# Holding back projections and starting products early in a planned order for a two-layer attention and GEGLU block

## The chip, the cores and the metric

The kernel runs on one core of one Trainium2 chip. The metric is the device time of one execution in microseconds (us), as the median of several runs. The profiled execution is a single one, taken by the hardware profiler, and its page gives a span from the first to the last instruction, a little shorter than the execution's time. Engines: PE is TensorE's matmul, PEld its weight load, DVE VectorE, ACT ScalarE, POOL GpSimd, SP SyncE (which here issues DMAs).

## The reference

Two layers over 2048 tokens of width 512, each an attention with a running memory followed by a GEGLU feed-forward. Both layers use the same weights.

```python
def _A_ref(x, wq, wk, wv, wo, beta):            # H = 32 heads of 16, N = 4 segments of L = 512 tokens
    q, k, v = ...                               # x @ wq, x @ wk, x @ wv, split by head and segment
    phi = lambda t: jnp.where(t > 0, t + 1.0, jnp.exp(t))
    g = _sigmoid(beta).reshape(1, H, 1, 1)
    M, z = 0, 0
    for s in range(N):
        p = _softmax(einsum('bhqd,bhkd->bhqk', qs, ks) * scale + mask)   # causal inside the segment
        a_dot = einsum('bhqk,bhkd->bhqd', p, vs)
        a_mem = (phi(qs) @ M) / (phi(qs) @ z + 1e-06)
        outs.append(g * a_mem + (1.0 - g) * a_dot)
        M = M + einsum('bhld,bhle->bhde', phi(ks), vs)
        z = z + phi(ks).sum(over l)
    return concat(outs) @ wo

def _B_ref(x, w_gate, w_up, w_down):            # F = 1792
    return _gelu(x @ w_gate) * (x @ w_up) @ w_down

x = A_x
for _ in range(2):
    x = x + _A_ref(_layernorm(x), A_wq, A_wk, A_wv, A_wo, A_beta)
    x = x + _B_ref(_layernorm(x), B_w_gate, B_w_up, B_w_down)
```

## The kernel before

The work is cut into eight pieces, called segments 1 to 8 here: segments 1 to 4 are the four segments of layer 1, 5 to 8 those of layer 2. In the code segment n has k = n - 1. Each runs through two classes. `Att(k)` makes the layer norm of its 512 tokens (tile `xnT`, the normed tokens transposed), the q, k and v products, the scores in 36 rounds, their exponentials, the products of probabilities and v (called flushes), and what the memory needs (`phi`, `mem`, `upd`). `Ffn(k)` makes the Wo product and adds it to x, the second layer norm, 14 gate tiles, 14 up tiles and the down product.

A product on TensorE is four matmuls over the four blocks of 128 of the contraction (14 for down), each with up to 512 columns, into one of eight PSUM banks (tile `ps`). Scores use TensorE in row tiles (four head groups at once), flushes in column tiles (four groups of 32 output columns). A dense product can be whole or cut in four column tiles, so that it can follow a flush without a change of tiling; a matmul in column tiles is then four instructions that run side by side.

The order of everything is made in advance, when the program is built. `order()` walks along a planned clock (`ck`), on which each engine has a time at which it is free. It keeps a list of items: an `Item` has a due time, a condition (`ready`) on what must be there by then, the matmuls to be issued (`ops`), and what follows on other engines (`done`). At each step the main loop does the first of these that it can: two score rounds, if ScalarE's list of exponentials runs low and two bank pairs are free; the next matmul of the item that is open; open the ready item with the least due time; score rounds regardless of ScalarE's list; a fill product of the constant tile `warm`; let 0.05 us pass on the planned clock. Each engine then runs its queue in that fixed order, with semaphores for what it needs from others, so on the chip a late operand holds up everything behind it on the same engine.

Due times, preferences and thresholds are numbers in the table `POLICY`, changed every 20 us of the planned clock by `STAGES`. Those that matter here: `quick`, for how many of the four token blocks after Wo the addition to x also gives the row sum, with the squares then summed on ScalarE (`Norm.added`, L750 to L757), in place of `bn_stats` on VectorE (L737); `turn_pe`, whether normed blocks are transposed by TensorE (L426, tiles `ident` and `xn`, then a copy out of PSUM) or by a DMA (L635); `direct`, how many gate tiles go through GELU straight from PSUM (L1385) rather than being copied to `gel_sb` first (L660 on ScalarE, L659 on VectorE) and put through GELU in place (L1468).

Nearly all matmuls are recorded at one line, L422. In the profile they are told apart by what they read: `wq_sb`, `wk_sb`, `wv_sb`, `aT,wo_sb`, `wg_sb` (gate), `wu_sb` (up), `gel_sb,wd_sb` (down), `q` with `kf` or `kx` (scores), `pt` with `vaug` or `vz` (flush). The exponentials are L1716 on ScalarE. From a flush to Wo, VectorE reads out and transposes (L1266), takes reciprocals (L1276), scales (L1282) and transposes back into `aT` (L1289); L1292 adds the memory's part. From Wo to the gates the path is: addition to x (L1338), statistics (L737, L740), one over the deviation (L777 and L783 on ScalarE or L775 and L780 on GpSimd), scaled block `xn` (L801), transpose into `xnT`.

Of the kernel before, what the change touches and what calls it, by code (L numbers as in the profile page):

```python
# [21 lines left out]
NSEG = 4  # L22
NK = 2 * NSEG
L = 512
# [41 lines left out]
def table(halved):  # L66
# [17 lines left out]
    if halved:  # L84
# [31 lines left out]
    rs_pool=2.183, f_urge=-172.366, quick=0, paired=2, turn_pe=1, turn_last=0, w_at=31.878, w_gap=1.658,  # L116
    wd_at=82.393, wd_gap=1.568, flush_wait=-24.125, piece_slack=54.103, kb_slack=137.385, mem_slack=-57.872,
    margin=0.5, qk_due=0.997, e_q=-0.936, e_k=1.44, exp_slack=-54.603, e_slack=89.377, phi_slack=25.941,
    gelu_slack=-0.515, act_evict=7.804, first_evict=59.504, gate_step=5.742, up_due=-13.195, up_step=36.193,
    down_due=-11.638, down_step=-8.082, upd_due=2.96, kb_act=13.215, vz_slack=-3.085, x_dve=18.716, v0_due=-19.099,  # L120
    x1_at=-0.749, x2_at=17.766, x3_at=25.618, x3_load=-134.921, direct=4, gelu_tiles=6, look=1.24, lag=0.479,
    wv_at=-163.476, xn_pool=70.356, kb_pool=58.307, cut_pool=-1.34, at_pool=-24.815, pe_turns=0, gate_due=-25.221,
    shun=2.375, col_gap=3.222, hold=14, early=1.718, starve=0.315, near=7.532, cap=8, soon=2.605, columns=0,
    kd_slack=-7.947, zero_slack=-2.858)
# [3 lines left out]
        f_urge=-142.106, turn_pe=0, kb_slack=136.166, e_q=-0.628, upd_due=0.734, gelu_tiles=4, cut_pool=-1.244)),  # L128
    (2, 3, dict(
        rs_pool=2.062, f_urge=-142.106, turn_pe=2, flush_wait=-23.401, kb_slack=132.867, qk_due=-4.716, e_q=-0.628,  # L130
        phi_slack=25.306, gelu_slack=3.249, act_evict=-10.809, down_due=-8.472, down_step=-19.183, upd_due=2.131,
        kb_act=8.112, vz_slack=-2.427, gelu_tiles=3, look=1.351, xn_pool=81.967, kb_pool=58.345, cut_pool=-1.308,
        at_pool=-4.617, gate_due=-26.901, shun=4.857, early=1.703, starve=0.32, near=7.708, soon=2.65)),
    (3, 4, dict(
        rs_pool=2.062, f_urge=-142.106, turn_pe=2, flush_wait=-23.401, kb_slack=132.867, qk_due=-4.716, e_q=-0.628,
        phi_slack=25.306, gelu_slack=3.249, act_evict=-10.809, gate_step=6.048, up_step=48.132, down_due=-8.472,
        down_step=-19.183, upd_due=2.131, kb_act=8.112, vz_slack=-2.427, x_dve=-17.494, gelu_tiles=3, look=1.351,
        xn_pool=81.967, cut_pool=-1.308, at_pool=-4.617, gate_due=-3.182, shun=4.857, hold=10, early=1.703,
        starve=0.32, near=7.708, cap=9, soon=2.65)),
    (4, 5, dict(  # L140
        rs_pool=6.739, f_urge=-142.106, quick=1, turn_pe=4, flush_wait=-25.073, piece_slack=89.739, kb_slack=132.867,
        mem_slack=-58.782, qk_due=-65.306, e_q=-0.628, e_k=5.331, exp_slack=-31.237, phi_slack=25.306,
        gelu_slack=3.249, act_evict=-10.809, gate_step=5.036, up_due=-0.982, up_step=0.332, down_due=-8.472,
        down_step=-19.183, upd_due=16.794, kb_act=1.607, vz_slack=-2.427, x_dve=-2.16, look=1.351, lag=0.415,
        xn_pool=-0.079, cut_pool=-1.491, at_pool=20.04, gate_due=10.318, shun=3.803, hold=10, early=1.703,
        starve=0.338, near=6.791, cap=12, soon=30.667)),
    (5, 6, dict(
        rs_pool=7.71, f_urge=-142.106, quick=1, paired=1, turn_pe=4, flush_wait=-32.146, piece_slack=89.739,
        kb_slack=132.746, mem_slack=-59.02, qk_due=-65.538, e_q=-0.535, e_k=5.331, exp_slack=-31.237,
        phi_slack=25.29, gelu_slack=3.249, act_evict=-10.809, gate_step=5.036, up_due=-0.982, up_step=0.332,  # L150
        down_due=-8.472, down_step=-18.931, upd_due=16.794, kb_act=-3.437, vz_slack=-2.427, x_dve=-2.16, direct=6,
        look=1.351, lag=0.415, xn_pool=-0.079, cut_pool=-1.491, at_pool=24.384, gate_due=1.419, shun=3.803, hold=9,
        early=1.703, starve=0.338, near=6.791, cap=13, soon=30.667)),
    (6, 7, dict(
        rs_pool=-35.334, f_urge=-142.106, quick=6, paired=1, turn_pe=8, flush_wait=-3.829, piece_slack=-11.221,
        kb_slack=105.872, mem_slack=73.299, qk_due=-8.214, e_q=-7.15, e_k=84.404, exp_slack=0.985, phi_slack=36.681,
        gelu_slack=139.816, act_evict=-10.809, gate_step=5.036, up_due=-0.571, up_step=0.208, down_due=74.558,
        down_step=-6.986, upd_due=-1.601, kb_act=120.49, vz_slack=-45.689, x_dve=6.382, gelu_tiles=7, look=2.788,
        lag=0.247, xn_pool=9.373, cut_pool=1.514, at_pool=24.384, gate_due=-0.563, shun=101.359, hold=11,
        early=1.703, starve=59.91, near=-2.703, cap=6, soon=-12.515)),  # L160
    (7, 8, dict(
# [292 lines left out]
def order(pol, nc, cst, seg, wrk, psp, A_x, A_wq, A_wk, A_wv, A_wo, A_beta, B_x, B_w_gate, B_w_up, B_w_down, out):  # L454
# [412 lines left out]
    class Att:  # L867
# [977 lines left out]
```

## Time and profile before

| | |
|---|---|
| median of 3 runs | 538.32 us (537.79 to 538.46) |
| profiled execution | 537.38 us |
| its span | 535.7 us |
| granted TensorE clock, mean | 1.000 |
| instructions on TensorE in the profile | 10403 matmuls, 10462 weight loads |
| exponentials on ScalarE (L1716) | 288, busy 280.2 us |
| multiplication of gate and up on VectorE (L1409) | 112, busy 74.3 us |
| SP's queue | 52 transposes of `xn`, 14 copies of `vaug` into `vz` |

How to read it: a group's line gives line, engine, operation, tiles, shapes and count, then busy time and the mean duration of one in ns, then idle time of the engine ahead of them with what ended most of it. A timeline line gives start, length, engine, line, operation, tiles, shapes and count of merged instructions, with idle time before them in brackets where there is some. A matmul's record lasts until its result is out, and the next one starts well before that, so the distance of starts is the time that a matmul takes from TensorE, not the record's length. A few matmul records are missing from the trace.

### The profile page before, as it was taken

The numbers are of one execution on the slowest core, as the hardware profiler recorded it, in microseconds if no ns is written. First come the engines' busy times: TensorE is split into PE (matmuls) and PEld (weight loads), VectorE is DVE, ScalarE is ACT, GpSimd is POOL, SyncE is SP. The second block draws the span as 40 slices with busy tenths as digits, with TensorE's granted clock in tenths as the row PEclk, the third lists the DMA queues.
The fourth block names the chain that finished last, engine by engine and source line by source line (L and its number), as shares of the span: only waits on it lengthen the run. The fifth ranks groups of instructions, "written<-read, shape, count | busy, mean of one in ns | idle before, by whom it ended". The sixth has DMA issues, their size and how long they took to land.

```text
span 535.7 us, 23633 instructions
## 1 busy us (share of the span) xinstructions
PE 518.7 (97%) x10403; PEld 272.4 (51%) x10462; DVE 438.7 (82%) x834; ACT 438.9 (82%) x589; POOL 275.2 (51%) x343
## 2 busy tenths in 40 slices
PE   8999989999999999999999999999999999999997
PEld 4455455545554445544555445444565456556554
DVE  7987998998888999888999899879887897685342
ACT  7999999989999889998699986998899978942320
POOL 2977585467872968727677167513563155300000
PEclk9999999999999999999999999999999999999999
DMA  8378841152121123310323123101230114003001
GB/s 267 70 101 207 183 130 33 23 64 50 23 53 31 24 42 53 61 24 2 72 42 62 24 42 62 23 0 23 61 64 2 23 32 82 15 2 71 12 2 42
DMA packets 74586, 29.46 MB, mean 55 GB/s; under 512 B 58866, under 2 KB 74482, under 8 KB 74482
## 3 DMA queue, kind: packets, MB, share of 16 engines
q1 hardware_dynamic: 74192, 27.67, 25.5%
q8 instruction: 82, 1.34, 1.0%
q10 hardware_dynamic: 290, 0.26, 0.1%
q14 instruction: 22, 0.18, 0.1%
HBM read 9.70 MB, written 2.10 MB: 22 GB/s over the span
## 4 chain that ended last, share of the span: by engine, by line
PE 85%; DVE 9%; issue 2%; ACT 2%; DMA 0%; POOL 0%; DVEq 0%; POOLq 0%
PE ps L422 84%; ACT pt L1716 2%; DVE byq L1266 1%; DVE x_sb L1338 1%; DVE e L1026 1%; DVE ab L1282 1%; DVE st L737 1%; DVE pt L1675 1%; DMA x_sb<-in_A_x_dram 0%; PE ps L426 0%; DVE gel_sb L1409 0%; DVE r L1276 0%; DVE aT L1289 0%; DVE st L1501 0%; DVE vaug L659 0%
## 5 line engine op out<-in xcount | busy, mean ns | idle before, releaser
L1716 ACT ACTIVATE pt<-ps 128x1024 bf16<-128x1024 f32 x288 | 280.2, 1036 | 37.9 <-PE ps L422 31.7
L1665 POOL TENSOR_SCALAR_AFFINE_SELECT pt<-pt 128x256 bf16<-128x256 bf16 (+1 forms) x192 | 111.5, 594 | 143.1 <-ACT pt L1716 127.3
L422 PE MATMUL ps<-xnT,wg_sb 128*32 128x512 bf16 (+1 forms) x1143 | 105.6, 380 | 2.0 <-issue 1.1
L422 PE MATMUL ps<-wd_sb,gel_sb 128*32 128x512 bf16 (+2 forms) x1486 | 102.4, 353 | 1.8 <-issue 1.6
L422 PE MATMUL ps<-xnT,wu_sb 128*32 128x512 bf16 (+1 forms) x1188 | 100.8, 379 | 1.3 <-issue 1.1
L1409 DVE TENSOR_TENSOR gel_sb<-gel_sb,ps 128x512 bf16<-128x512 bf16 x112 | 74.3, 683 | 25.7 <-PE ps L422 22.7
L422 PEld LDWEIGHTS <-gel_sb 128*32 128x32 bf16 (+1 forms) x1689 | 53.5, 97 | 40.8 <-issue 1.5
L422 PEld LDWEIGHTS <-wu_sb 128*32 128x32 bf16 (+1 forms) x1198 | 44.6, 97 | 46.9 <-issue 0.9
L422 PEld LDWEIGHTS <-wg_sb 128*32 128x32 bf16 (+1 forms) x1156 | 43.0, 97 | 42.8 <-issue 0.7
L1266 DVE STREAM_TRANSPOSE byq<-ps 128x512 f32<-128x512 f32 x64 | 45.1, 706 | 17.4 <-PE ps L422 17.0
L1045 POOL TENSOR_SCALAR e<-e 128x512 bf16<-128x512 bf16 x34 | 52.9, 1558 | 2.7 <-ACT e L1022 2.0
L1338 DVE TENSOR_TENSOR x_sb<-x_sb,ps 128x512 bf16<-128x512 bf16 (+1 forms) x59 | 37.1, 639 | 20.5 <-PE ps L422 19.7
L1670 POOL TENSOR_SCALAR_AFFINE_SELECT pt<-pt 64x1024 bf16<-64x1024 bf16 x38 | 45.8, 1205 | 11.2 <-ACT pt L1716 7.0
L422 PE MATMUL ps<-pt,vaug 128*32 128x256 bf16 (+2 forms) x1344 | 34.9, 238 | 0.8 <-POOL pt L1665 0.5
L1468 ACT ACTIVATE gel_sb<-gel_sb 128x512 bf16<-128x512 bf16 (+4 forms) x42 | 35.3, 928 | 0.0
L422 PE MATMUL ps<-xnT,wq_sb 128*32 128x512 bf16 (+2 forms) x261 | 34.3, 377 | 0.8 <-issue 0.5
L737 DVE BATCH_NORM_STATS2 st<-x_sb 128x6 f32<-128x512 bf16 x51 | 34.5, 677 | 0.1
L422 PE MATMUL ps<-xnT,wk_sb 128*32 128x512 bf16 (+2 forms) x263 | 33.4, 376 | 1.0 <-issue 0.5
L659 DVE CAST gel_sb<-ps 128x512 bf16<-128x512 f32 x45 | 30.0, 679 | 4.9 <-PE ps L422 4.5
L422 PEld LDWEIGHTS <-vaug 128*32 128x32 bf16 x1344 | 27.4, 97 | 10.2 <-issue 1.8
L422 PE MATMUL ps<-wv_sb,xnT 128*32 128x512 bf16 (+1 forms) x223 | 30.9, 380 | 0.7 <-issue 0.5
L422 PE MATMUL ps<-q,kx 32*128 32x64 bf16 (+2 forms) x1120 | 31.1, 217 | 0.5 <-ACT pt L1716 0.4
(128 smaller groups left out, 701.6 us busy)
## 6 DMA issues: line engine op xcount, KB each, us to landing
vz<-vaug SPq DMA_DIRECT2D x14, 136.0 KB, 2.9
wg_sb<-in_B_w_gate_dram SPq DMA_DIRECT2D x8, 224.0 KB, 4.4
wu_sb<-in_B_w_up_dram SPq DMA_DIRECT2D x8, 224.0 KB, 3.5
wd_sb<-in_B_w_down_dram SPq DMA_DIRECT2D x7, 256.0 KB, 5.8
x_sb<-in_A_x_dram SPq DMA_DIRECT2D x3, 512.0 KB, 7.2
out_dram<-x_sb SPq DMA_DIRECT2D x12, 128.0 KB, 1.9
xnT<-xn SPq DMA_TRANSPOSE x52, 2.5
kx<-kf SPq DMA_DIRECT2D x12, 64.0 KB, 4.4
```

Of the source, the lines that this page charges most:

```text
L422: self.nc.tensor.matmul(*args, **kw)
L659: ck.dve.post(ck.made(), slack, (0.673, lambda: nc.vector.tensor_copy(out=dst(), in_=src()), end), taken=taken)
L737: nc.vector.bn_stats(out=self.st6[:, 0, :], in_=x_sb[:, self.tt0 + j, :])
L1026: nc.vector.scalar_tensor_tensor(out=dst, in0=src, scalar=0.0, in1=e[0][:], op0=ALU.max, op1=ALU.add, accum_out=self.zk[:, b:b + 1] if whi ...
L1045: lambda eng: eng.tensor_scalar(out=e[0][:], in0=e[0][:], scalar1=1.0, scalar2=None, op0=ALU.min), summed)
L1266: nc.vector.transpose(out=(self.byq[:, pars[0], :, :].rearrange("p a c -> p (a c)") if h is None else self.byq[:].rearrange("p u a c -> p ...
L1338: ck.dve.post(ck.made(), slack, (0.15 + 0.00104 * (c1 - c0), lambda: nc.vector.tensor_tensor(out=xt, in0=xt, in1=ps()[:, 0:c1 - c0], op=AL ...
L1409: ck.dve.post(ck.made(), NORMAL, (0.683, lambda: nc.vector.tensor_tensor(out=g, in0=g, in1=ps()[:], op=ALU.mult), lambda t: (ps.read(t), e ...
L1468: return (0.205 + 0.427 * (f1 - f0), lambda: nc.scalar.activation(out=g, in_=g, func=ACT.Gelu_apprx_tanh), lambda t: self.gelu_done(t, f0, ...
L1665: nc.gpsimd.affine_select(out=view, in_=view, pattern=[[0, 4], [0, n], [1, C]], compare_op=ALU.is_ge, fill=0.0, base=C, channel_multiplier=-1)
L1670: nc.gpsimd.affine_select(out=view, in_=view, pattern=[[0, 4 * TPS], [1, C]], compare_op=ALU.is_ge, fill=0.0, base=0, channel_multiplier=-1)
L1716: nc.scalar.activation(out=pt_all[:, s0:s0 + 2, 2 * p:2 * p + 2, :].rearrange("p r h c -> p h r c"), in_=ps_all[:, pair[0]:pair[1] + 1, :] ...
```

## The change

Four things change. First, the q and k items of segments 2 to 4 (`0 < k < NSEG`) are not ready before a given round of scores has been issued, and neither are their v items; the round is set by `hold1`, `hold2`, `hold3` for the segment, `hold_step` for the block, and `hold_v` more for v. Second, a Wo item can be begun when three of its four head blocks are there, once all scores of its segment are issued: three matmuls now, the item is then parked with its bank, and the last matmul follows when the fourth block is there. Third, a gate item can be begun when the first two token blocks of `xnT` are there: four matmuls on 256 columns, the item is parked, and four more on the other 256 columns follow. Both are tried only where no item is ready and no score round can be issued, that is where the loop came to a fill before, and at most `park` items are parked. Parked items go on ahead of any other. Fourth, all numbers of `POLICY` and `STAGES` are new, with a stage for nearly each 20 us.

```diff
 POLICY = dict(
-    rs_pool=2.183, f_urge=-172.366, quick=0, paired=2, turn_pe=1, turn_last=0, w_at=31.878, w_gap=1.658,
...
+    kd_slack=-5.85, zero_slack=-1.031, hold1=-49.923, hold2=2.205, hold3=11.541, hold_step=-162.485, hold_v=23.995,
+    park=3)
...
+        self.early, self.rest, self.stop = None, None, 0
...
+            def begun_by(j, more=0.0):
+                if not 0 < k < NSEG:
+                    return True
+                now = STEPS * streams[0][0] + streams[0][1] if streams else 1e9
+                return now >= (0.0, pol.hold1, pol.hold2, pol.hold3)[k] + pol.hold_step * j + more
...
-                return Item(lambda: k - pol.qk_due + 0.01 * b, lambda: storage() and ck.has(("xnTa", k)), dense(ps, pairs),
+                return Item(lambda: k - pol.qk_due + 0.01 * b, lambda: storage() and begun_by(b) and ck.has(("xnTa", k)), dense(ps, pairs),
...
-                            lambda: ck.has(("xnTa", k, j)) and (k or ck.pe > max(pol.wv_at, 13.4)) and
+                            lambda: ck.has(("xnTa", k, j)) and begun_by(j, pol.hold_v) and (k or ck.pe > max(pol.wv_at, 13.4)) and
...
+                def early():
+                    if ("scores", k) in ev and soon(("aTh", k, j // 2), KT - 1, eager=True):
+                        it.stop = 1
+                        return True
+                    return False
+
+                it.early, it.rest = early, lambda: ck.has(("aTh", k, j // 2, KT - 1), by=ck.pe - 0.1)
...
+                def early():
+                    if not (ck.has(("xnTf", k, 0), ("xnTf", k, 1)) and free()):
+                        return False
+                    it.ops[:] = [(Clocks.MM[512] / 2, lambda i=i, l=l, r=r, c=c: product(ps()[:, c], l(), r()[:, c], i == 0, i == KT - 1))
+                                 for c in (slice(0, L // 2), slice(L // 2, L)) for i, (l, r) in enumerate(pairs)]
+                    it.stop = KT
+                    return True
+
+                it.early, it.rest = early, lambda: ck.has(("xnTf", k))
...
-            if not opened.ops:
+            if len(opened.ops) == opened.stop:
                 it, opened = opened, None
-                it.done()
+                if it.ops:
+                    parked.append(it)
+                else:
+                    it.done()
+            continue
+        got = [it for it in parked if it.rest()]
+        if got:
+            opened = got[0]
+            opened.stop = 0
+            parked.remove(opened)
             continue
...
+        if bank is not None and len(parked) < pol.park:
+            got = [it for it in sorted((it for it in items if it.early), key=lambda it: it.due())[:6] if it.early()]
+            if got:
+                opened = open_item(got[:1], bank)
+                continue
```

What the built programs hold, by count of instructions:

| | before | after |
|---|---|---|
| fill products after the start (whole / in column tiles) | 25 / 20 | 11 / 8 |
| transposing matmuls of `xn` on TensorE | 48 | 32 |
| transposes of `xn` by DMA | 52 | 56 |
| gate matmuls on 256 columns (whole / in column tiles) | 0 / 0 | 31 / 196 |
| changes of TensorE's tiling along its queue | 298 | 294 |
| additions to x with a row sum, squares on ScalarE | 9 | 14 |
| products read out into `gel_sb` by ScalarE, GELU or copy | 68 | 76 |
| v tiles read out into `vaug` by ScalarE / VectorE | 9 / 19 | 16 / 12 |
| GELU in place on ScalarE (instructions / tiles) | 42 / 70 | 31 / 68 |

All other products have the same number of columns in total. Three Wo items of segment 2 and three of segment 8 are begun on three head blocks, and ten gate items, in segments 3 and 4, on 256 tokens.

More of the change, by code (lines that the diff above doesn't have):

```diff
@@ L1393, in done, with free @@
                         self.gelu_all(ck.pe)
-                return Item(lambda: -0.8 if phase[0] == k else k + pol.gate_due + pol.gate_step * place(ft),
-                            lambda: ck.has(("xnTf", k), ("loaded", "first")) and (k == 0 and ft >= HELD or (("down", k - 1) if k else ("upd", 0)) in ev),
-                            dense(ps, pairs), done, kind="gate", ps=ps, after=("xnTf", k))
+                def free():
+                    return ck.has(("loaded", "first")) and (k == 0 and ft >= HELD or (("down", k - 1) if k else ("upd", 0)) in ev)
+                it = Item(lambda: -0.8 if phase[0] == k else k + pol.gate_due + pol.gate_step * place(ft),
+                          lambda: ck.has(("xnTf", k)) and free(),
+                          dense(ps, pairs), done, kind="gate", ps=ps, after=("xnTf", k))
+                def early():
[6 more added lines that the diff above has]
+                it.early, it.rest = early, lambda: ck.has(("xnTf", k))
+                return it
             def up(ft):
@@ L1592, in order @@
     streams = [(k, t) for k in range(NK) for t in range(STEPS)]
-    opened = None
+    opened, parked = None, []
     score_banks = set()
```

288 lines of the change are left out of this document (203 added, 85 removed).

## The prediction

> **What bounds the kernel now.** I read the page first, then busy time by stage, then TensorE's instructions in order of time where the stages showed idle time. The page's lines on the span, the busy shares, the granted clock and the chain that ended last:
>
> ```profile
> span 535.7 us, 23633 instructions
> PE 518.7 (97%) x10403; PEld 272.4 (51%) x10462; DVE 438.7 (82%) x834; ACT 438.9 (82%) x589; POOL 275.2 (51%) x343
> PEclk9999999999999999999999999999999999999999
> PE 85%; DVE 9%; issue 2%; ACT 2%; DMA 0%; POOL 0%; DVEq 0%; POOLq 0%
> ```
>
> TensorE holds 85% of the chain and runs at full clock in every slice. In 17.0 us of the span (535.7 less 518.7) no matmul is running. The profiled execution took 537.38 us, 1.7 us more than its span; the median of the three runs is 538.32, 0.94 above it. I work out a difference on the profiled execution and apply it to the median. About 0.2%, 1.1 us, is the smallest difference that a measurement of this kernel can tell from none.
>
> Busy time by stage:
>
> ```profile
> 20.00:40.00 20.00, 19.01 (x369) 9.60 (x374) 17.16 (x40) 20.00 (x28) 16.66 (x24) 1.00 0.61 89
> 60.00:80.00 20.00, 17.77 (x407) 10.05 (x406) 19.40 (x40) 18.59 (x24) 13.95 (x19) 1.00 0.58 136
> 100.00:140.00 40.00, 37.92 (x828) 19.90 (x823) 36.98 (x75) 35.95 (x54) 30.46 (x32) 1.00 0.27 39
> 140.00:180.00 40.00, 39.22 (x843) 20.71 (x848) 33.85 (x63) 39.27 (x50) 23.96 (x28) 1.00 0.18 36
> ```
>
> The columns after the length are PE, PEld, DVE, ACT, POOL. TensorE is idle for 2.23 us in 60 to 80 and 2.08 us in 100 to 140, and hardly elsewhere. In 60 to 80 VectorE is busy for 19.40 of 20; ScalarE is full in 20 to 40 and nearly so (39.27 of 40) in 140 to 180. So TensorE bounds the kernel, with two places where it waits, and ScalarE stands close behind it.
>
> Busy shares flatter TensorE, because a record runs on after the next matmul has started. So I read starts. TensorE's timeline at those places; `ps<-warm` are the fill products, put in where the planner has no work ready:
>
> ```profile
> 63.50 0.33 PE L422 MATMUL ps<-warm 128*128 128x128 bf16 x3
> 63.76 0.41 PE L422 MATMUL ps<-q,kx 32*128 32x64 bf16 x20
> ...
> 70.18 0.28 PE L422 MATMUL ps<-warm 128*32 128x128 bf16 x8
> ...
> 71.28 0.40 PE L426 MATMUL ps<-ident,xn 128*128 128x128 bf16 x4
> ...
> 72.04 0.23 PE L422 MATMUL ps<-warm 128*128 128x128 bf16 x1
> 72.40 0.40 PE L426 MATMUL ps<-ident,xn 128*128 128x128 bf16 x4
> 72.63 0.42 PE L422 MATMUL ps<-warm 128*128 128x128 bf16 x4
> ...
> 73.64 0.29 PE L422 MATMUL ps<-q,kf 16*128 16x64 bf16 x8
> ...
> 75.27 0.62 PE L426 MATMUL ps<-ident,xn 128*128 128x128 bf16 x8
> 75.72 0.33 PE L422 MATMUL ps<-warm 128*128 128x128 bf16 x3
> ...
> 76.47 1.02 PE L422 MATMUL ps<-xnT,wg_sb 128*128 128x512 bf16 x3
> ...
> 107.81 1.03 PE L422 MATMUL ps<-xnT,wu_sb 128*128 128x512 bf16 x4 [0.16 <-issue]
> 108.67 0.44 PE L422 MATMUL ps<-warm 128*128 128x128 bf16 x5
> 109.04 0.28 PE L422 MATMUL ps<-q,kx 32*128 32x256 bf16 x2
> 109.75 0.40 PE L422 MATMUL ps<-q,kx 32*128 32x256 bf16 x10 [0.42 <-ACT pt L1716]
> ...
> 134.93 0.39 PE L422 MATMUL ps<-warm 128*128 128x128 bf16 x4
> ...
> 135.78 0.38 PE L422 MATMUL ps<-xnT,wg_sb 128*128 128x512 bf16 x1 [0.46 <-ACT xnT L660]
> ```
>
> From the first fill of each stretch to the next useful start I read 0.26, 1.10, 0.36, 1.01, 0.75, 0.37 and 0.85 us: 4.70 us in which TensorE does nothing of use. Of the program's 30 fills (25 whole, and 20 instructions that make five groups of four) 29 lie in these stretches, so a fill stands for 0.162 us of dead time. The stretches from 70 to 76 are the layer norm after the first Wo products: their blocks wait for VectorE.
>
> **The change part by part.** *Dead time.* The new order has 13 fills (11 whole, two groups). The v products of segment 4 now stand behind the first Wo products, where before only fills and scores stood, and VectorE's chain there loses two statistics. Sixteen v products are 16 x 0.215 = 3.4 us of cover (four matmuls from 107.81 to 108.67), against the 3.48 us of dead time up to 76.47. In segment 2 the q, k and v products of segment 5 take the place of the fills at 134.93. At 0.162 each, 17 fewer fills give **-2.8 us**. Ends: -4.7 if all dead time goes, 0 if each wait stays and only its fill goes.
>
> *Transposes.* TensorE turns 48 blocks of 128 columns before and 32 after. Eight of them take from 75.27 to 75.72, 0.056 us each: 16 x 0.056 = **-0.9 us**. Four token blocks go to the DMA queue instead. There one takes longer, so cover matters; that is the cover term below.
>
> *Tiling.* A turn between row tiles (scores), column tiles and whole products costs a pause: the five fills from 108.67 are worth 0.28 us at that rate, and the score round starts after 0.37, so 0.09. The program has 298 turns before and 294 after: **-0.4 us**.
>
> *Gates on 256 tokens.* Ten gate tiles are made in two halves: 80 products of 256 columns for 40 of 512. The last products of the program have that width:
>
> ```profile
> 529.79 2.14 PE L422 MATMUL ps<-wd_sb,gel_sb 128*32 128x256 bf16 x72
> ```
>
> Here 18 groups of 256 columns take 2.14 us with a tail of some 0.16 us: 0.110 each, so two halves cost 0.220 against 0.215, **+0.1 us** (40 x 0.005 = 0.2 at most). [...]
>
> *Wo begun on three head blocks, and the wait that this adds.* This happens in segments 2 and 8, for three token blocks each. TensorE takes its queue in order: if the fourth head block is late, everything behind the parked product waits. In segment 8, 56 `up` products stood between the last flush and Wo, and now eight, followed by nine Wo products on three blocks: 17 x 0.215 = 3.7 us until the fourth is needed. The chain to it on VectorE (read-out, reciprocal, scaling, transpose, addition):
>
> ```profile
> L1266 DVE STREAM_TRANSPOSE byq<-ps 128x512 f32<-128x512 f32 x64 | 45.1, 706 | 17.4 <-PE ps L422 17.0
> L1276 DVE RECIPROCAL r<-byq 128x32 f32<-128x32 f32 x32 | 11.3, 354 | 1.1
> L1282 DVE TENSOR_TENSOR ab<-byq,r 128x512 bf16<-128x512 f32 x32 | 24.7, 770 | 1.1
> L1289 DVE STREAM_TRANSPOSE aT<-ab 128x512 bf16<-128x512 bf16 x32 | 22.5, 705 | 0.6
> L1292 DVE TENSOR_TENSOR aT<-aT,amT 128x512 bf16<-128x512 bf16 x11 | 5.0, 458 | 0.2
> ```
>
> That is 2.99 us beside hand-overs, with 0.7 to spare. VectorE also multiplies the `up` tiles there; one such multiplication in the way uses that up. Between 0 and +0.7 I take **+0.2 us**. Queued behind the wait are the rest of Wo and the last `down` products, so it would come out in full.
>
> *Cover of the norm in segments 3 and 4.* From the last Wo product to the first gate there were 42 and 56 `down` products before; now 28 and 28, and the gates start on two token blocks. What the chain needs, from segment 4 before:
>
> ```profile
> 246.56 2.34 PE L422 MATMUL ps<-wo_sb,aT 128*32 128x512 bf16 x40
> 254.05 5.52 SPq L635 DMA_TRANSPOSE xnT<-xn  x4
> xnT<-xn SPq DMA_TRANSPOSE x52, 2.5
> ```
>
> The first row opens with block 1 (16 instructions, done 0.86 us on, at 247.4). Its transpose is issued second of four, 1.38 us after 254.05, and lands 2.5 us later, at 257.9: 10.5 us from Wo to usable. In the new order I count, by the rates above, 9.6 us of products from Wo of block 1 to the first gate of segment 3, and 10.1 in segment 4. Taken at face value that is 0.9 + 0.4 = 1.3 us of new waiting; at best 0, if VectorE puts less of its other work between. Its queue is laid out afresh, so I stay below the middle: **+0.4 us**.
>
> Order rows that these terms rest on. VectorE at the norm of segment 1, before, from the first addition of Wo to x (L1338) to the second scaled block (L801):
>
> ```order
> L1338 TENSOR_TENSOR x_sb<-x_sb,ps 128x512
> L737 BN_STATS st_1554<-x_sb 128x6
> L740 BN_AGGR mv<-st_1554 128x2
> L1338 TENSOR_TENSOR x_sb<-x_sb,ps 128x512 x2
> L737 BN_STATS st_1585<-x_sb 128x6
> L740 BN_AGGR mv<-st_1585 128x2
> L737 BN_STATS st_1697<-x_sb 128x6
> L740 BN_AGGR mv<-st_1697 128x2
> L1338 TENSOR_TENSOR x_sb<-x_sb,ps 128x512
> L801 TENSOR_SCALAR xn<-x_sb,mv,rs 128x512
> ```
>
> and after (L869 adds with a row sum, L873 makes the mean):
>
> ```order
> L869 SCALAR_TENSOR_TENSOR x_sb,rowsum<-ps,x_sb 128x512
> L873 TENSOR_TENSOR mv<-rowsum,means 128x2
> L869 SCALAR_TENSOR_TENSOR x_sb,rowsum<-ps,x_sb 128x512
> L873 TENSOR_TENSOR mv<-rowsum,means 128x2
> L1463 TENSOR_TENSOR x_sb<-x_sb,ps 128x512
> L856 BN_STATS st_1529<-x_sb 128x6
> L859 BN_AGGR mv<-st_1529 128x2
> L1463 TENSOR_TENSOR x_sb<-x_sb,ps 128x512
> L920 TENSOR_SCALAR xn<-x_sb,mv,rs 128x512 x2
> ```
>
> Two of four blocks leave their squares to ScalarE, and two scaled blocks leave VectorE after eight instructions instead of one after ten. TensorE behind the last Wo product of segment 1, before:
>
> ```order
> L422 MATMUL ps<-wo_sb,aT 128x512
> L422 LDWEIGHTS warm
> L422 MATMUL ps<-warm 128x128
> L422 LDWEIGHTS phik
> L422 MATMUL ps<-gel_sb,phik 32x32
> ```
>
> and after:
>
> ```order
> L541 LDWEIGHTS aT
> L541 MATMUL ps<-wo_sb,aT 128x512
> L541 LDWEIGHTS xnT
> L541 MATMUL ps<-wv_sb,xnT 128x512
> L541 LDWEIGHTS xnT
> ```
>
> The v products, which stood ahead of Wo, now follow it.
>
> The sum: -2.8 - 0.9 - 0.4 + 0.1 + 0.2 + 0.4 = -3.4 us, so 534.9.
>
> **The rivals.** *ScalarE takes over (slower).* The new order gives ScalarE eight more products to read out into the gate tile, seven more v tiles, five more squares:
>
> ```profile
> L660 ACT ACTIVATE gel_sb<-ps 128x512 bf16<-128x512 f32 x29 | 16.9, 612 | 1.2 <-PE ps L422 1.1
> L660 ACT ACTIVATE vaug<-ps 128x512 bf16<-128x512 f32 x9 | 5.8, 672 | 0.0
> L757 ACT ACTIVATE junk<-x_sb,mv 128x512 bf16<-128x512 bf16 x9 | 6.5, 720 | 8.3 <-DVE mv L754 8.2
> L1468 ACT ACTIVATE gel_sb<-gel_sb 128x512 bf16<-128x512 bf16 x31 | 17.3, 641 | 0.0
> L1468 ACT ACTIVATE gel_sb<-gel_sb 128x1024 bf16<-128x1024 bf16 x3 | 3.2, 1075 | 0.0
> ```
>
> That is 8 x 0.612 + 7 x 0.672 + 5 x 0.720 = 13.2 us. GELU in place falls from 42 instructions on 70 tiles to 31 on 68: by the last two rows a second tile adds 0.434 and an instruction has 0.207 on top, so 11 x 0.207 + 2 x 0.434 = 3.1 us go. Net +10.1 us. Where ScalarE is full (20 to 40, 140 to 180) each such microsecond delays an exponential, the flush that needs it and the bank that the next score needs. If all of it came through: 534.9 + 10.1 = 545.0; half of it 540.0. It decides once ScalarE has no wait for TensorE left. For it: those two stages. Against it: ScalarE is busy for only 82% and has 96.8 us to spare, and the order puts 80 of its instructions instead of 84 ahead of the last exponential of segment 1. [...] Chance 0.16.
>
> *The waits only move.* The fills go, but the operands come no earlier, and TensorE stands without a fill instead. Then -2.8 falls away: 538.32 - 0.6 = 537.7. For it: fills are only the planner's mark of a wait. Against it: the cover of 3.4 us is real work moved there. Chance 0.15.
>
> *More waits go.* The new order may clear all dead time, 1.9 us more than the forecast's 2.8, and waits without a fill, like the 0.7 us from 109.04 to 109.75, where two of four score tiles start and the others wait for an exponential: 534.9 - 1.9 - 0.7 = 532.3. For it: the wait at 134.93 sits in a norm that now has 44 products of segment 5 beside it. Against it: 13 fills are left in the order. Chance 0.19.
>
> **How the numbers follow.** The forecast, 534.9, has 0.50; about 1.5 us either way by the ends of its terms. Faster by over 0.2% holds for the forecast, for the rival with more waits gone and for a quarter of "only move": 0.50 + 0.19 + 0.04 = 0.73. The rest of that rival, 0.6 us from no change, is no difference: 0.11. Slower is ScalarE: 0.16. The range reaches from 531.7 (below "more waits go" by the 0.6 us of new waits in the sum) to 538.3 ("only move", with 0.6 us more of them) and leaves out ScalarE's case.
>
> **What would show it.** Right: the 60 to 80 stage of the new profile loses about 2 us of TensorE's idle time; the small `ps<-warm` instructions fall from 45 to 19 and their stretches sum to about 2.1 us; `ident` has 32 matmuls, 0.9 us less; no wait over 0.5 us at the gates of segments 3 and 4. Wrong: waits of TensorE for `pt L1716` or for gate and v tiles read out by ScalarE that add up to over 4 us (ScalarE), waits for `xnT` at the gates of segments 3 and 4 above 1.3 us (cover), a wait for `aT` at the last Wo above 0.7, or 256-column gate products that start more than 0.12 us apart.

## The result and the profile after

| | before | after |
|---|---|---|
| median of nine runs | 537.79 us (537.04 to 538.69) | 536.35 us (536.04 to 537.07) |
| profiled execution / its span | 537.38 / 535.7 us | 536.81 / 535.1 us |

The ratio is 0.9974, 95% interval 0.9964 to 0.9984: faster by 1.4 us, where 3.4 us were forecast. The time lies in the predicted range, but less than half of the gain came. The page's lines on the span, the busy shares, the clock and the chain that ended last, after:

```profile
span 535.1 us, 24177 instructions
PE 525.1 (98%) x10697; PEld 276.3 (52%) x10697; DVE 433.7 (81%) x823; ACT 445.9 (83%) x598; POOL 268.1 (50%) x333
PEclk9999999999999999999999999999999999999999
PE 77%; DVE 4%; ACT 3%; POOL 1%; issue 1%; DMA 0%; ACTq 0%
```

TensorE still bounds the kernel; ScalarE took on 7.0 us and did not take over. Busy time by stage, after (columns after the length: PE, PEld, DVE, ACT, POOL):

```profile
20.00:40.00 20.00, 19.68 (x380) 9.95 (x382) 17.98 (x38) 19.90 (x30) 17.67 (x22) 1.00 0.52 105
60.00:80.00 20.00, 18.52 (x372) 9.94 (x366) 18.76 (x39) 17.66 (x30) 12.35 (x13) 1.00 0.62 167
100.00:140.00 40.00, 37.97 (x832) 18.86 (x832) 38.12 (x73) 33.14 (x46) 30.77 (x35) 1.00 0.32 54
140.00:180.00 40.00, 39.78 (x793) 20.73 (x792) 35.33 (x64) 39.33 (x49) 17.13 (x23) 1.00 0.22 37
```

In 60 to 80 TensorE's idle time fell from 2.23 to 1.48 us, and in 100 to 140 it is 2.03 where it was 2.08. These two stages were to bring the gain. Most of their fills did go. TensorE's timeline with the stretches of fills from 68 to 71, after (L541 is the product, L545 the transpose):

```profile
68.89 0.33 PE L541 MATMUL ps<-warm 128*128 128x128 bf16 x3
69.07 0.40 PE L545 MATMUL ps<-ident,xn 128*128 128x128 bf16 x4
69.30 0.22 PE L541 MATMUL ps<-warm 128*128 128x128 bf16 x1
69.39 0.34 PE L545 MATMUL ps<-ident,xn 128*128 128x128 bf16 x3
...
70.50 0.55 PE L541 MATMUL ps<-warm 128*128 128x128 bf16 x7
71.08 0.28 PE L541 MATMUL ps<-gel_sb,phik 128*32 128x32 bf16 x17
```

These three take 0.18, 0.09 and 0.58 us; with two groups of column tiles later (0.23 and 0.16) the dead stretches sum to 1.24 us. All eight stretches of before sum to 4.99. In their place stand waits without a fill, on TensorE's timeline after:

```profile
74.92 0.29 PE L541 MATMUL ps<-q,kf 16*128 16x64 bf16 x7
76.20 0.36 PE L541 MATMUL ps<-q,kf 16*128 16x192 bf16 x5 [0.99 <-issue]
...
124.24 0.83 PE L541 MATMUL ps<-wo_sb,aT 128*32 128x512 bf16 x12 [0.21 <-issue]
...
127.94 1.68 PE L541 MATMUL ps<-wo_sb,aT 128*128 128x512 bf16 x7
131.44 0.81 PE L541 MATMUL ps<-wv_sb,xnT 128*128 128x512 bf16 x3 [1.82 <-DVE x_sb L1463]
...
199.78 1.27 PE L541 MATMUL ps<-xnT,wg_sb 128*32 128x256 bf16 x36 [0.30 <-DMA xnT<-xn]
```

I laid TensorE's starts one behind the other, took off what each product's columns need (0.215 us for 512), and so read each wait start to start: 1.16 us at 76.20, 0.38 at 124.24, 1.98 at 131.44 and 0.47 at 199.78. The first two carry no semaphore ("issue"). The first lies inside a round of scores, between the third and the fourth of four products that need the same things.

**Place 1: 76.20.** What the DMA queues moved from 71.20 to 73.90 (queue, packets, MB, share of the 16 engines), after:

```profile
q1 hardware_dynamic: 720, 0.70, 81.1%
```

and from 73.90 to 74.95:

```profile
q1 hardware_dynamic: 334, 0.33, 91.1%
q8 instruction: 1, 0.02, 5.6%
```

Queue 8 brings TensorE's own program, 16,384 bytes at a time: the page counts 83 of its transfers, one for each 258 of the 21,394 matmuls and weight loads. This transfer ran from 73.96 to 74.90, and TensorE went on 1.30 us later. The one for 124.24 ended at 122.85, 1.39 us before. Counted from the start of TensorE's program the two stopped instructions are 2499 and 4547: 9 x 256 + 195 and 17 x 256 + 195. I call these places the program's borders. By the same count TensorE passed the border at 8 x 256 + 195 at 71.24. The transfer for the stop at 76.20 began 2.72 us after that; no other in this profile began more than 1.54 us behind the border before it.

**Place 2: 131.44.** TensorE waits for the bank of a Wo product, which the first addition to x (L1463) frees. VectorE's timeline there, after:

```profile
126.62 1.29 DVE L920 TENSOR_SCALAR xn<-x_sb,mv,rs 128x512 bf16<-128x512 bf16 x1
127.83 1.09 DVE L1305 TENSOR_TENSOR zacc<-zacc,zk 128x4 f32<-128x4 f32 x1
128.84 0.40 DVE L920 TENSOR_SCALAR xn<-x_sb,mv,rs 128x512 bf16<-128x512 bf16 x1
129.17 1.62 DVE L1286 TENSOR_TENSOR mblk<-macc,bd 128x512 bf16<-128x512 f32 x1
130.71 1.87 DVE L1463 TENSOR_TENSOR x_sb<-x_sb,ps 128x512 bf16<-128x512 bf16 x3
```

and GpSimd's:

```profile
126.61 1.15 POOL L1417 TENSOR_TENSOR aT<-aT,amT 128x512 bf16<-128x512 bf16 x1 [0.31 <-DVE aT L1414]
127.72 2.53 POOL L1818 TENSOR_SCALAR_AFFINE_SELECT pt<-pt 64x1024 bf16<-64x1024 bf16 x2
```

The same scaling of a block (L920) takes 1.29 us beside GpSimd's addition and 0.40 two rows on; an addition of four numbers a row takes 1.09. The three Wo products begun early hold their banks until VectorE is through with this.

### The profile page after: what moved, and what is told of

It reads as the page before. It is cut to its first block, busy times and chain, and to the rows that moved or that the text cites. A ratio compares the mean times of both kernels' runs of the same rounds, so it can differ in the third digit from the quotient of the medians.

```text
span 535.1 us, 24177 instructions
## 1 busy us (share of the span) xinstructions
PE 525.1 (98%) x10697; PEld 276.3 (52%) x10697; DVE 433.7 (81%) x823; ACT 445.9 (83%) x598; POOL 268.1 (50%) x333
## 4 chain that ended last, share of the span: by engine, by line
PE 77%; DVE 4%; ACT 3%; POOL 1%; issue 1%; DMA 0%; ACTq 0%
PE ps L541 77%; ACT pt L1864 1%; ACT gel_sb L1616 1%; POOL kx L726 1%; DVE xn L920 1%; ACT gel_sb L1519 1%; POOL e L1170 1%; ACT gel_sb L779 0%; DMA xnT<-xn 0%; DVE x_sb L1463 0%; DVE st L856 0%; DVE mblk L1286 0%; DVE byq L1391 0%; DVE x_sb L869 0%; ACT L1519 0%
## 5 line engine op out<-in xcount | busy, mean ns | idle before, releaser
L541 PE MATMUL ps<-xnT,wg_sb 128*32 128x512 bf16 (+3 forms) x1367 | 107.7, 362 | 0.3 <-DMA xnT<-xn 0.3
L541 PE MATMUL ps<-wd_sb,gel_sb 128*32 128x512 bf16 (+2 forms) x1431 | 106.1, 354 | 0.0
L541 PE MATMUL ps<-xnT,wu_sb 128*32 128x512 bf16 (+1 forms) x1252 | 103.6, 379 | 0.2 <-ACT gel_sb L1519 0.2
L541 PEld LDWEIGHTS <-gel_sb 128*32 128x32 bf16 (+1 forms) x1623 | 53.2, 97 | 41.2 <-issue 2.2
L541 PEld LDWEIGHTS <-wu_sb 128*32 128x32 bf16 (+1 forms) x1252 | 45.8, 97 | 45.3 <-issue 2.0
L541 PEld LDWEIGHTS <-wg_sb 128*32 128x32 bf16 (+1 forms) x1367 | 47.5, 97 | 38.7 <-issue 1.5
L1170 POOL TENSOR_SCALAR e<-e 128x512 bf16<-128x512 bf16 x32 | 50.0, 1565 | 7.1 <-ACT e L1147 6.4
L1463 DVE TENSOR_TENSOR x_sb<-x_sb,ps 128x512 bf16<-128x512 bf16 (+1 forms) x54 | 34.0, 635 | 17.8 <-PE ps L541 17.7
L1818 POOL TENSOR_SCALAR_AFFINE_SELECT pt<-pt 64x1024 bf16<-64x1024 bf16 x32 | 38.1, 1192 | 17.8 <-ACT pt L1864 15.6
L541 PE MATMUL ps<-xnT,wk_sb 128*32 128x512 bf16 (+2 forms) x330 | 34.9, 377 | 0.7 <-ACT pt L1864 0.7
L541 PE MATMUL ps<-pt,vaug 128*32 128x256 bf16 (+2 forms) x1344 | 35.1, 239 | 0.1
L541 PE MATMUL ps<-wv_sb,xnT 128*32 128x512 bf16 (+1 forms) x227 | 32.4, 380 | 2.2 <-DVE x_sb L1463 1.8
L541 PE MATMUL ps<-xnT,wq_sb 128*32 128x512 bf16 (+2 forms) x339 | 34.0, 377 | 0.0
L1616 ACT ACTIVATE gel_sb<-gel_sb 128x1024 bf16<-128x1024 bf16 (+4 forms) x31 | 33.3, 1157 | 0.0
L541 PE MATMUL ps<-q,kx 32*128 32x64 bf16 (+2 forms) x1120 | 31.4, 217 | 0.6 <-ACT pt L1864 0.3
L541 PEld LDWEIGHTS <-vaug 128*32 128x32 bf16 x1344 | 27.2, 97 | 9.2 <-issue 1.6
L856 DVE BATCH_NORM_STATS2 st<-x_sb 128x6 f32<-128x512 bf16 x46 | 31.2, 679 | 0.4
L541 PEld LDWEIGHTS <-kx 32*128 32x128 bf16 x1120 | 16.8, 92 | 28.1 <-issue 27.4
```

The costliest lines, as they stand in the source:

```text
L541: self.nc.tensor.matmul(*args, **kw)
L856: nc.vector.bn_stats(out=self.st6[:, 0, :], in_=x_sb[:, self.tt0 + j, :])
L1170: lambda eng: eng.tensor_scalar(out=e[0][:], in0=e[0][:], scalar1=1.0, scalar2=None, op0=ALU.min), summed)
L1463: ck.dve.post(ck.made(), slack, (0.15 + 0.00104 * (c1 - c0), lambda: nc.vector.tensor_tensor(out=xt, in0=xt, in1=ps()[:, 0:c1 - c0], op=AL ...
L1616: return (0.205 + 0.427 * (f1 - f0), lambda: nc.scalar.activation(out=g, in_=g, func=ACT.Gelu_apprx_tanh), lambda t: self.gelu_done(t, f0, ...
L1818: nc.gpsimd.affine_select(out=view, in_=view, pattern=[[0, 4 * TPS], [1, C]], compare_op=ALU.is_ge, fill=0.0, base=0, channel_multiplier=-1)
```

## Experiments

Ratios are to the kernel before in runs on the same chip. The account of stops by instruction number is from each run's trace. Taken singly, the intervals of spread1, adds and masks overlap that of the changed kernel (0.9964 to 0.9984), so for these three the profiles carry the argument and not the ratio.

**The changed kernel again** (no edit).

> The changed kernel itself once more, with a second profile. If the stops are the program's and not one execution's: 1.1 to 1.3 us near 76.2 and 0.4 near 124.2 again, both at instruction 195 of a stretch of 256, and 1.9 to 2.0 us near 131.4 again; ratio 0.9974 (0.9964 to 0.9984) as before. If they are one execution's, they differ by more than 0.5 us.

Measured: 0.9981 (0.9966 to 0.9996). Its profile has 1.07 us at 76.13, 0.38 at 124.15 (both at instruction 195 again) and 1.99 at 131.36. The waits belong to the program, not to one execution.

**Moving the borders.** More, narrower opening products, with the same work behind them:

```
-    keep_warm(WARM, 0)
+    for n in range(92):                      # shift2: 105, 56 columns
+        (te if n < WARM else nc.tensor).matmul(ps_all[:, 0, 0:64], lhsT=warm[:], rhs=wide[:, 0, 0:64], ...)
```

> The changed kernel with 92 narrow opening products (64 columns) in place of 12 wide ones (512 columns): 160 instructions more on TensorE's queue before the first transpose, the same work behind them. Theory 'code': the two stops of TensorE in the changed kernel that begin in the middle of its queue without a semaphore (1.17 us at 76.20 inside a round of scores, 0.40 us at 124.24) are waits for the next 16 KB of TensorE's program, whose transfer ended 1.30 and 1.38 us before TensorE went on; moved by 160 instructions, the borders of 256 instructions fall where TensorE takes over 5 us for 140 products, and both stops go. The first is then worth 1.2 us; the second may be eaten by the wait for the adds at 131.44. Ratio to before 0.9952 (0.9943 to 0.9957). Rival 'banks': the stop at 76.20 is a wait for VectorE's late read of a bank (75.29 to 75.97); nothing changes: ratio 0.9974, the stop stays.

Measured: 1.0010 (0.9997 to 1.0022), 1.9 us over the changed kernel. The stop at 124.24 is gone, the one at 76.20 is shorter and further on, and two are new: the one at 407.53 below, and 0.38 us at 273.68. TensorE's timeline of shift:

```profile
77.39 0.29 PE L541 MATMUL ps<-pt,vz 128*32 128x64 bf16 x13 [0.28 <-issue]
...
125.69 1.04 PE L541 MATMUL ps<-wv_sb,xnT 128*128 128x512 bf16 x3 [0.91 <-DMA xnT<-xn]
...
407.53 0.20 PE L541 MATMUL ps<-vaug,phik 128*32 128x32 bf16 x2 [0.85 <-issue]
```

The rows at 77.39 and 407.53 begin with instructions 10 x 256 + 195 and 63 x 256 + 195 (the second is a matmul whose weight load, the 194th, had gone through), and 273.68 is 41 x 256 + 195. So the stop is at the border of the program and not at a bank. The theory's time was wrong: the new places of the borders cost as much, 1.86 us in three stops against 1.54 in two. The loss of 1.9 us is not these stops; the profile has waits for transposes, the longest at 125.69, and 0.65 us for a load of `wq` at 12.50, and what brought them was not tried.

> As shift, with 105 opening products of 56 columns: 186 instructions more in place of 160. In four runs so far every stop without a semaphore stands at instruction 194 or 195 of a stretch of 256 on TensorE's queue, 1.12 to 1.46 us after a transfer of 16 KB ended, and shift only moved the borders to other quick places (0.45 us at 77.39, 1.03 us at 407.53). Theory 'code': with 186 the times of the changed kernel put every border where at least 3.3 us pass from instruction 150 of one stretch to 195 of the next, 5 us while weights are loaded; only a stop of about 0.1 us is left (near 124.5). The stops of 1.16 and 0.38 us go, the wait for the adds at 131.44 takes up the second: 1.2 us under the changed kernel, ratio 0.9952. Rival 'any shift costs': stops come back elsewhere, ratio 0.997 to 1.001.

Measured: 0.9990 (0.9976 to 1.0004). The stops behaved as forecast but for one of 0.45 us at 76.81. Yet waits for transposes came, and no time was won. TensorE's timeline of shift2:

```profile
125.10 1.04 PE L541 MATMUL ps<-wv_sb,xnT 128*128 128x512 bf16 x4 [0.67 <-DMA xnT<-xn]
...
199.36 0.84 PE L541 MATMUL ps<-xnT,wg_sb 128*32 128x256 bf16 x24 [0.63 <-DMA xnT<-xn]
...
267.89 0.83 PE L541 MATMUL ps<-xnT,wg_sb 128*128 128x256 bf16 x6 [1.21 <-DMA xnT<-xn]
```

**The same in the kernel before**, with 52 opening products of 116 columns.

> The kernel before, with 52 opening products of 116 columns for 12 of 512: 80 instructions more ahead of the rest, the same work. Theory 'code': by the times of before, the borders then fall where too little time passes from instruction 150 of one stretch to 195 of the next: 3.9 us near 71.8 (weights are loaded, 5 are wanted), 3.13 near 207.6 and 2.61 near 267.6 (3.4 are wanted); stops of TensorE at instruction 195 within 2 us of two or more of these places, 1.5 to 2.2 us in all, ratio 1.003 to 1.004. Rival: where the borders fall costs nothing by itself, ratio 1.000 and no stop without a semaphore.

Measured: 1.0088 (1.0071 to 1.0105), 4.7 us slower. TensorE's timeline of bshift:

```profile
73.66 0.36 PE L422 MATMUL ps<-q,kf 16*128 16x192 bf16 x5 [1.46 <-issue]
...
210.92 0.28 PE L422 MATMUL ps<-q,kx 32*128 32x256 bf16 x3 [0.81 <-issue]
...
271.88 0.20 PE L422 MATMUL ps<-vaug,phik 128*32 128x32 bf16 x2 [0.87 <-issue]
```

Three stops at the three places foretold, 1.62 + 0.97 + 1.04 = 3.6 us, larger than the 2.2 expected, each at instruction 195 of its stretch. The count from instruction 150 and the times wanted, there (3.4 and 5 us) and in shift2 (3.3 and 5), were estimates of mine; the runs show the stops and no such limit. Where the borders fall costs time by itself. But the stops are not the whole of the 4.7 us. TensorE's dead time took up 0.8 us of the first one, and 2 us after it the granted clock (the third column from the end) was at half for 3.4 us:

```profile
75.70:79.10 3.40, 3.18 (x55) 2.46 (x49) 2.81 (x7) 3.19 (x5) 1.25 (x3) 0.51 0.00 0
79.10:82.00 2.90, 2.90 (x24) 1.12 (x22) 2.66 (x5) 2.40 (x4) 2.17 (x2) 0.99 0.00 0
```

By the starts of the same weight loads in the profiles of before and of bshift, this stretch cost 1.1 us. All six executions of bshift have a mean clock of 0.993 to 0.997; of the 17 of before beside them 13 have 0.998 or more.

**Making the transfer early without moving the borders.** Loads of the down weights are sent later on SP's queue; the order of the other four engines is untouched:

```
+            if h >= 3:                       # spread1: 1
+                piece = lambda h=h, piece=piece: wd_later.append((95.0 + 0.6 * (h - 3), piece))
...
+        while wd_later and wd_later[0][0] <= ck.pe:
+            wd_later.pop(0)[1]()
```

> The changed kernel with the last four of the seven loads of the down weights behind the first transposes of amT on SP's queue, so that three and not six of 256 KB are sent at 69.5 us; the other four engines' order is the same to the instruction. Theory: the transfer of TensorE's program at 73.96 began 2.7 us after the border before it because six weight loads lay ahead of it (the median of all such transfers is 0.2 to 0.3 us behind the border); with three it begins by 72.6, and the stop of 1.16 us at 76.20 falls under 0.3: ratio 0.9955 (0.9950 to 0.9962). Rival: the delay has another cause, the stop stays, ratio 0.9974; or the four loads are late for the down products at 106, a stop there of 1 us or more.

Measured: 0.9987 (0.9966 to 1.0008); the stop is 1.24 us. The transfer came at 73.60, as the three loads drained, only 0.36 us earlier. The three loads that the changed kernel issues at 71.22, 71.69 and 72.20, as TensorE passes the border at 71.24 and behind it, were worth no more than that.

> As spread, with one load of the down weights left at 69.5 us and six behind the first transpose of amT (spread left three, and TensorE's program still came at 73.60, when those three had drained). Theory: the transfer of the program, asked for near 71.1, waits behind what was sent before it; behind one load it begins by 72.4, and the stop near 76.2 falls from 1.16 to 0.2 us or less; the down products find their weights, which land by 103. Ratio 0.9955, and 0.9964 if 0.5 us of it comes back. Rival: the delay is not from the loads; the transfer begins at 73.5 or later again, the stop stays, ratio 0.9974.

Measured: 0.9958 (0.9942 to 0.9973). The transfer of the program stands alone in the DMA's time from 72.40 to 73.40, in spread1:

```profile
q8 instruction: 1, 0.02, 5.8%
```

That is 1.56 us earlier than the 73.96 of the changed kernel, with two loads fewer ahead of it than in spread. TensorE's timeline of spread1 has no stop at the border:

```profile
74.83 0.40 PE L541 MATMUL ps<-q,kf 16*128 16x64 bf16 x12
75.16 1.05 PE L541 MATMUL ps<-xnT,wg_sb 128*32 128x512 bf16 x16
...
200.98 1.27 PE L541 MATMUL ps<-xnT,wg_sb 128*32 128x256 bf16 x36 [2.57 <-DMA xnT<-xn]
```

The cause of place 1 is shown. The last row is a wait that the profiled execution of spread1 has (537.96 us, its median is 536.02): the transpose issued at 196.52 landed 4.42 us later, and a transfer of the program began at 198.53.

**VectorE's queue at place 2.** The additions of Wo go ahead of zacc and mblk:

```
-                             (0.154, lambda: nc.vector.tensor_tensor(out=zacc[:], ...
+                             (0.154, later(lambda: nc.vector.tensor_tensor(out=zacc[:], ...
-                ck.dve.chain(..., (Port(0.69), spread, None), (Port(0.2), z, told))
+                ck.dve.chain(..., (Port(0.69), later(spread), None), (Port(0.2), z, told))
```

where `later` holds the call in segment 2 until three additions are issued.

> The changed kernel with one thing moved on VectorE: in the second segment the three adds of Wo's products to x are issued ahead of the add to zacc and the making of mblk, not behind them; the order elsewhere is the same. Theory 'VectorE's queue': TensorE's wait of 1.98 us at 131.44 for the first add goes, since the add can begin at 128.0 and end 0.8 us before TensorE comes to it; mblk is read only after zcols, which stands far behind, so nothing else gets late: ratio 0.9938 (0.9930 to 0.9950). Rival 'the waits only move': TensorE stops at the next thing that is late, the read-outs behind or the exponentials, and at least half of the 1.98 us comes back within 20 us: ratio 0.9956 to 0.9974.

Measured: 0.9959 (0.9945 to 0.9973), 0.8 us under the changed kernel. TensorE's timeline of adds:

```profile
127.89 1.69 PE L541 MATMUL ps<-wo_sb,aT 128*128 128x512 bf16 x7
129.67 1.46 PE L541 MATMUL ps<-wv_sb,xnT 128*128 128x512 bf16 x6
```

The wait fell from 1.98 to 0.26 us; 0.66 of it came back at 136.6 and 137.5, where TensorE waits for ScalarE. By the starts of the same weight loads in both profiles, adds is 1.72 us further ahead of the changed kernel past 131.4 than it was at 126, and 0.90 us at 140.0. Nearly half was back within 9 us, and the ratio lies in the rival's range.

**GpSimd's part in place 2.** The two half masks of that round go to VectorE as one instruction:

```
+        halves_of.append(slot)
+        if len(halves_of) in (11, 12):
+            if h == 0:
+                mask_both(slot)
+            return
```

> The changed kernel with the two half masks that GpSimd makes at 127.72 (2.53 us) made by VectorE as one instruction between mblk and the three adds (0.67 us by its other instances). Theory 'shared': the add to zacc (1.09 us there, 0.15 to 0.29 elsewhere) and mblk (1.62, 0.7 elsewhere) were long because GpSimd ran beside them; without it they take 0.15 and 0.7, the adds begin 0.94 + 0.92 - 0.67 = 1.2 us earlier, and the wait of 1.98 us at 131.44 falls to 0.8: ratio 0.9952. Rival 'queue alone': their length has another cause (waits of their own); VectorE has 0.67 us more ahead of the adds, the wait grows to 2.6 us: ratio 0.9987.

Measured: 0.9951 (0.9934 to 0.9969). VectorE's timeline of masks (L1830 is the mask):

```profile
128.25 0.39 DVE L1305 TENSOR_TENSOR zacc<-zacc,zk 128x4 f32<-128x4 f32 x1
128.56 0.40 DVE L920 TENSOR_SCALAR xn<-x_sb,mv,rs 128x512 bf16<-128x512 bf16 x1
128.88 0.68 DVE L1286 TENSOR_TENSOR mblk<-macc,bd 128x512 bf16<-128x512 f32 x1
129.49 0.68 DVE L1830 TENSOR_TENSOR pt<-pt,tri 128x1024 bf16<-128x1024 bf16 x1
```

and TensorE's:

```profile
130.82 1.45 PE L541 MATMUL ps<-wv_sb,xnT 128*128 128x512 bf16 x6 [0.90 <-DVE x_sb L1463]
```

With 0.68 us more to do, VectorE is earlier: zacc falls from 1.09 to 0.39, mblk from 1.62 to 0.68, the wait from 1.98 to 1.06. GpSimd's instruction beside them made them long.

**Both places at once.** With the shifted borders:

> The edits of shift and adds together. If the two kinds of stop are what ate the gain and do not cover one another, the gains add up: 1.2 + 1.9 and the 0.4 us at 124.24, 3.1 to 3.5 us under the changed kernel, near 533.0, where the prediction was 534.9: ratio 0.9913 (0.9905 to 0.9925). If the waits only move, 0.9940 or more.

Measured: 0.9995 (0.9977 to 1.0012). The profile has stops of 1.02, 1.32 and 1.72 us at 52.30, 79.35 and 409.13, again at instruction 195 of their stretches: what adds wins, the borders lose. With the loads sent later instead:

> adds and spread1 together. If the stops add up: 1.0 us at 76.2, 0.4 at 124.2 that no longer hides behind the adds' wait only as far as the chain there lets it (counted 0), and 0.8 to 1.7 us of the adds: 534.1 to 534.9, ratio 0.9932 to 0.9945. If what one frees another takes, 0.9955 or more.

Measured: 534.68 us (534.62 to 535.34), ratio 0.9929 (0.9915 to 0.9943). This beats both kernels, 3.8 us under before and 2.4 us under the changed one by the ratios. TensorE's timeline of two runs through the border of place 1 and waits 0.30 us at place 2:

```profile
75.02 0.40 PE L541 MATMUL ps<-q,kf 16*128 16x64 bf16 x12
...
126.99 1.69 PE L541 MATMUL ps<-wo_sb,aT 128*128 128x512 bf16 x7
128.81 1.46 PE L541 MATMUL ps<-wv_sb,xnT 128*128 128x512 bf16 x6
```

The gain that was forecast was there; the two waits had taken 2.4 us of it.

**The parts.** The new numbers without early starts, and the early starts with the numbers of before:

```
-        if bank is not None and len(parked) < pol.park:      # nopark
+        if bank is not None and len(parked) < 0:
```

> The changed kernel's numbers with no early start (neither Wo on three head blocks nor gates on 256 tokens); the planner makes another order of it, with 59 fills in place of 13. Theory 'one design': the numbers were chosen with the early starts, and each of the 46 fills more is a hole of about 0.216 us that the planner had nothing for: 10 us more than the changed kernel, 546 (542 to 550), ratio 1.015. Rival 'the early starts do little': under 2 us, ratio 0.998 to 1.001.

> The early starts alone: the changed program with the numbers of before (with no early start these give the program of before, instruction for instruction) and up to three begun products. The order gets 96 fills in place of 30. Theory 'one design': 66 fills more of 0.216 us, 14 us slower than before, 552 (545 to 558), ratio 1.026. Rival 'the early starts help by themselves', as the terms for Wo and the gates would have it, at most 1 us either way: ratio 0.996 to 1.002.

Measured: nopark 1.0206 (1.0189 to 1.0223), oldnum3 1.0338 (1.0320 to 1.0355). Neither part gains with the rest as it is; numbers chosen for one part alone were not tried. Each fill more goes with the same loss in both: 12.5 us over the changed kernel for 46, 0.27; 17.9 us over before (538.34 to 556.24) for 66, 0.27. This is not the price of a fill alone, because both profiles also have stretches of 3.4 us at half the granted clock, one in nopark (from 273.9) and three in oldnum3 (from 75.0, 211.5 and 221.7). The third part, keeping q, k and v back, does next to nothing: the program without it has the same instructions in the same order on all five engines, but that two token blocks of v in segment 2 change places.

## Why the prediction was wrong, step by step

*Dead time, -2.8.* The step was right in kind and too small: the stretches went from 4.99 to 1.24 us, -3.75. The prediction had read 4.70, one stretch fewer, and expected 2.1 to be left.

*Transposes, tiling, gates: -0.9, -0.4, +0.1.* They held. Summed over the program by columns and turns, TensorE's own work falls by 2.14 us, of which 0.95 is the 17 fills' own time. A turn into or out of row tiles leaves 0.09 to 0.10 us in the profile after (101 turns without a semaphore), as the term had it. Halves of 256 columns start 0.110 us apart (mean of 72; at most 0.12).

*Wo on three head blocks, +0.2, and cover, +0.4.* The fourth head block was waited for nowhere in segment 8. The gates of segment 3 waited 0.47 us (0.38 in the second profile) and those of segment 4 not at all. Both terms held where they were read. But three Wo products are begun early in segment 2 as well, and there the Wo term had no wait at all: place 2, 1.98 us.

*The step that failed* is that the sum allowed 0.6 us of new waits and looked for them only at the norm and at the late head block. Start by start, waits away from fills grew from 14.3 to 19.2 us, 4.9 more. Four places make 4.7 of that: 1.16 + 0.38 at the program's borders, 1.98 at VectorE behind the early Wo products, 0.47 at the gates, 0.7 in 25 to 50, where ScalarE is full and TensorE waits three times for an exponential (0.39, 0.42, 0.43 us; before once, 0.53). The rival "the waits only move" had no place or price for the first two. I read each "issue" wait as nothing, since the profile names nothing there; and I took durations on VectorE from means, while beside GpSimd's masks zacc took 1.09 us and not 0.39, and mblk 1.62 and not 0.68. That the early start of the three Wo products is what made their banks scarce at place 2 is argued from the order; no run left these three out alone. That 536.35 still lies in the range is partly luck: the dead time gave 0.95 us more than its term, which hid as much of the new waits.

By this account the profiled executions should differ by almost nothing; their spans differ by 0.6 us and the medians by 1.4. Single executions of one kernel spread over 1 us (the nine of the result) to 4.5 us (the twelve of the second run), so the account tells places, not the last microsecond.

*ScalarE takes over* did not come: TensorE's waits for exponentials are 2.4 us in all (1.24 in 25 to 50 and 1.13 in three later ones), and 0.4 for a gate tile, under the 4 us set. Whether the 0.7 us at the start can be had as well was not tried.

## What to carry to other kernels

When a plan replaces idle slots by work, sum the gain, then ask for each place what is late next: which buffers the early work holds, and whose queue frees them. A wait of TensorE that the profile lays to "issue" in the middle of like instructions is worth a count: if its instruction number repeats modulo 256, as it did in the 25 stops here (195 each time), look at what the DMA queues carried in the 3 us before (at 76.20 the transfer of the program began 2.72 us after TensorE had passed the border before, behind weight loads issued from 69.54 on). An order that is tuned so finely is tuned to where its program's borders fall as well: with 80 more instructions in the opening, the kernel before stopped at three borders for 3.6 us and came out 4.7 us slower (bshift).

## What the runs showed of the hardware

*TensorE's program comes in pieces of 256 instructions.* Behind the opening, the profiles of the changed kernel and of the twelve experiments have 25 stops of 0.3 us or more without a semaphore. In all of them the first instruction that is late is the 195th of a stretch of 256, and TensorE went on 1.1 to 1.5 us after a transfer of 16,384 bytes ended. The n-th transfer goes with the border at n x 256 + 195: in all fourteen profiles, before's included, it ended at least 1.12 us before TensorE came to that instruction. Why the borders lie at 195 and not at 0 is not shown. With column tiles four loads and four products stand for one, and the 256 instructions ahead of the stop at 124.24 were used up in 2.5 us (121.34 to 123.84).

*A transpose by DMA takes longer beside such a transfer.* From 80 us on, over 12 profiles, `xnT` landed 2.48 us (median of 307) after its issue with no transfer of the program in flight and 3.88 (118) with one. A slow transpose meets a transfer more easily, so the sorting itself may make some of the difference; sorted by whether a transfer ran in the first 2.4 us after the issue, the medians are 2.44 (204) and 3.46 (221). This was seen, not tried by itself; it is what I hold against shift and shift2.

*Two of VectorE's instructions took longer beside GpSimd's.* An addition of 128x4 (zacc) took 1.09 us and mblk 1.62 us beside GpSimd's two half masks (127.72 to 130.25 in the changed kernel); in masks, without them, they took 0.39 and 0.68. A scaling between the two (128.84) took 0.40 in both. Why the one is longer and the other not, no run shows.

*The granted clock can stand at half for 3.4 us.* Five such stretches lie inside the fourteen profiles, 3.41 us each: one in bshift, one in nopark, three in oldnum3. In bshift eight transposes took 0.104 us each (from 76.49 to 77.32) where before's took 0.056. All five lie beside waits of TensorE of 0.65 us or more, but the 1.98 us of place 2 brought none; what sets one off was not tried.
